# Attention prompt kernel: the last 512 tokens transposed by DMA, with the order of the start and the planner's table changed

## The chip, the core and the metric

The kernel runs on one core of one Trainium2 chip. The metric is the device time of one execution in microseconds: 803.9 us before the change, the median of three runs (802.73 to 804.06). TensorE (PE) multiplies, VectorE (DVE) and ScalarE (ACT) work element by element, GpSimd (POOL) helps, SyncE (SP) issues nearly all DMAs. Every engine runs its own list of instructions in order, and semaphores make one wait for another.

## What is computed

The inputs are x (2048 tokens of 640), two sets of weights and a gate vector, all bf16. Attention A is full softmax attention with 32 heads of 20; attention B is a local one, in which each token looks at 8 tokens at distances 0, 2, ... 14 before it. The result mixes both with a gate for each token. Cut to what matters:

```python
x = A_x
g = sigmoid((x * gate_w).sum(-1, keepdims=True))
# A: q, k, v = heads of x @ A_wqkv;  softmax(q k^T * 20**-0.5) v, heads joined, @ A_wo
# B: the same with B_wqkv, but keys and values only at s, s-2, ..., s-14; @ B_wo
out = g * A(x) + (1 - g) * B(x)
```

## The kernel before, in words

**Main loop.** A group is 512 queries of four heads (32 groups). For each group and each of 16 key blocks of 128 there are four score units, one for each head: 2048 units of 128 keys by 512 queries. Units are gathered into tiles of two or three. `qk` (L1616, matmuls L1629) fills a score buffer for a tile, `exp` (L1649, L1652) takes the exponential on ACT into one of five ebuf buffers, `pv` (L1661, matmuls L1693) multiplies with V into obank. Part of the units go round ACT: they ride along with a tile of two in its third bank, and DVE computes their exponential (L1642, then three shifts at L866 for a sum of four powers); such units come in quads of four (`wanted`, L1505, decides on each). There are two score buffers of three banks (`score[0]`, `score[1]`); the third bank of each, with a bank of its own called side 0, forms the pool of three side banks that all other matmul work shares. A tile of three units, or a tile with a rider, needs the third bank of its buffer.

**Planner.** The program is laid out by a planner that runs while it is built. `T(...)` puts a task with an estimated length on an engine's list; the estimates decide in which order tasks are placed, and nothing else. Between tiles, `spend` and `run_side` (L1284) take work from generators in order of priority: the V projection (`gen_v`, L762), K and Q projections of the other heads (`gen_kd`, `gen_qd`, `gen_q1`), constants such as KMd (`constants`, L515), the gate, attention B, the output folds. Where PE has nothing else, `filler` (L1700, matmuls L1714) inserts matmuls without use. `PLAN` (L50) is a table by tile number: at tile s it sets 21 parameters (slack, priorities, when to take a rider, filler share).

**The start, written out by hand.** SP issues the loads in this order: x in four parts of 512 tokens (the first in two halves), with wk0 (the K weights of the first four heads) after the first and wq0 (the Q weights of the first four heads) after the last, then WvA, WkA, gwT. x arrives with tokens on partitions and is needed with channels on partitions (`xT`). For every part `turn` (L1313, L1321) transposes on PE, 20 blocks of 128 by 128, into a score buffer, and `x_out` (L1334) evacuates it: ACT takes two of the five channel blocks (L1338), DVE three (L1341). `k_first` (L1355, L1348) projects K of the first four heads for one part, `k_max` (L1360, L1362) takes the maximum on DVE, `k_out` (L1366, L1369) writes kT on ACT. `q_half` (L1420, L1423) projects the queries of the first group; POOL pads their weights first (L558). The maxima of the four parts give a bound that enters the query by one more matmul (L1442, L1444). `v_first` and `v_out` (L1372, L1380) project V of the first key block into side 0 and copy it to vA on DVE. Then the generators start; `gen_v` (matmuls L592, copy L773) begins with block 1, since `NV0` is 1.

The banks for K by part are side 0, obank, side 0, and the third bank of score[1]. The B weights go into `stage` (L1461), over the space where the fourth part of x had landed.

Of the kernel before, what the change touches and what calls it, by code (L numbers as in the profile page):

```python
# [10 lines left out]
ALU = mybir.AluOpType  # L11
# [3 lines left out]
P = 128  # L15
S = 2048
D = 640
# [316 lines left out]
def _build(ctx, nc, A_x, A_wqkv, A_wo, B_wqkv, B_wo, gate_w, out):  # L334
# [33 lines left out]
    NE = 5  # L368
    NR = 2
    VW = TOK + 8  # L370
    NV0 = 1
    xT = sb([P, CN, S], BF16, "xT")
    WqP = sb([P, CN, P], BF16, "WqP")
    kvw = sb([P, 3 * CN * D], BF16, "kvw")
# [1515 lines left out]
```

## Time and profile before

| what | value |
|---|---|
| three runs, median (lowest, highest) | 803.9 us (802.73, 804.06) |
| profiled execution, own time | 802.24 us |
| its span in the profile | 800.4 us |
| ACT busy | 779.5 us (97%) |
| PE busy | 770.4 us (96%) |
| DVE busy | 717.6 us (90%) |
| POOL busy | 143.6 us (18%) |
| granted PE clock | 1.0 throughout |
| first exponential starts | 18.46 us |
| last exponential starts | 791.5 us |
| DMA share, 0 to 20 us | 0.95 |

Times inside the profile count from the start of the span. A line of the timeline gives start, length, engine, source line, operation, output and inputs by name, shape, how many were merged (x20) and, in brackets, the idle time before it with what ended it. A busy PE is not a PE at its peak, because matmuls are pipelined and their ends are modelled. SP's issuing and waiting are not counted as busy.

### The profile page before, as it was taken

Reading aid. Unit: us, or ns where it says so; the run is one execution under the profiler, and the core shown is the slowest. Engines: PE = TensorE matmul, PEld = TensorE weight load, DVE = VectorE, ACT = ScalarE, POOL = GpSimd, SP = SyncE. Lnnn points to the kernel's source line nnn. Section 1 sums busy time; section 2 is a strip of 40 time slices with the busy share of each in tenths; the row PEclk is TensorE's granted clock in tenths of the full one; section 3 lists DMA queues with packets and bytes.
Section 4 is the critical chain, followed back from the end, with each engine's and each line's share of the span. In section 5 each row is a group of like instructions: output and inputs, shape, how many; then the busy total and the mean of one; then the engine's idle time right before and its main releaser. Section 6 shows DMA issues by size and latency. Waiting matters only on the chain.

```text
span 800.4 us, 29142 instructions
## 1 busy us (share of the span) xinstructions
PE 770.4 (96%) x12193; PEld 274.6 (34%) x12194; DVE 717.6 (90%) x1291; ACT 779.5 (97%) x785; POOL 143.6 (18%) x239
## 2 busy tenths in 40 slices
PE   9999999999999999999999999999999999999997
PEld 5332223233333333432333334233333233333232
DVE  7567989999879999899989979999999988999995
ACT  5999999999999999999999999999999999999996
POOL 5004111105511211111111111111112111211110
PEclk9999999999999999999999999999999999999999
DMA  9101101012111301300122023022003001303001
GB/s 310 48 16 38 34 18 41 11 33 65 32 36 27 82 20 27 71 16 22 38 70 43 9 50 69 17 61 51 14 22 79 16 26 41 76 6 71 14 7 36
DMA packets 59446, 35.24 MB, mean 44 GB/s; under 512 B 25252, under 2 KB 58116, under 8 KB 59316
## 3 DMA queue, kind: packets, MB, share of 16 engines
q1 hardware_dynamic: 59028, 33.05, 16.7%
q8 instruction: 97, 1.59, 0.9%
q14 instruction: 33, 0.27, 0.1%
q10 hardware_dynamic: 288, 0.33, 0.1%
HBM read 11.45 MB, written 2.62 MB: 18 GB/s over the span
## 4 chain that ended last, share of the span: by engine, by line
PE 50%; ACT 30%; issue 12%; DVE 7%; ACTq 0%; DVEq 0%
ACT ebuf L1652 30%; PE score L1629 17%; PE obank L1693 14%; PE side L592 9%; PE score L592 4%; DVE uD L1642 3%; DVE uD L866 1%; PE side L1714 1%; PE obank L1714 1%; PE score L1321 1%; PE obank L493 1%; PE side L1050 1%; DVE stage L1036 0%; PE score L1714 0%; PE side L954 0%
## 5 line engine op out<-in xcount | busy, mean ns | idle before, releaser
L1652 ACT ACTIVATE ebuf<-score 128x1024 bf16<-128x1024 f32 (+1 forms) x750 | 766.9, 1192 | 4.7 <-PE score L1629 3.6
L1629 PE MATMUL score<-qT,kT 32*128 32x512 bf16 x2048 | 304.6, 384 | 21.3 <-ACT ebuf L1652 15.8
L1642 DVE TENSOR_SCALAR uD<-score 128x512 int16<-128x512 f32 x380 | 254.0, 680 | 23.7 <-PE score L1629 22.3
L866 DVE TENSOR_SCALAR uD<-uD 128x2048 int16<-128x2048 int16 x285 | 195.0, 701 | 7.0 <-PE obank L1693 6.3
L1629 PEld LDWEIGHTS score<-qT,kT 32*128 32x128 bf16 x2048 | 73.3, 91 | 275.7 <-ACT ebuf L1652 214.1
L1693 PE MATMUL obank<-ebuf,vA 128*21 128x512 bf16 x1668 | 164.8, 386 | 0.3 <-DVE oTt L806 0.2
L857 POOL TENSOR_TENSOR vS<-vA,vw 128x252 bf16<-128x252 bf16 x95 | 58.2, 613 | 472.1 <-DVE uD L866 320.4
L1693 PE MATMUL obank<-uD,vS 128*21 128x512 bf16 x1140 | 100.3, 380 | 0.0
L592 PE MATMUL side<-xT,kvw 128*32 128x256 bf16 (+1 forms) x1830 | 78.8, 284 | 0.2 <-DVE rQ L1015 0.2
L1693 PEld LDWEIGHTS obank<-ebuf,vA 128*21 128x21 bf16 x1668 | 40.8, 88 | 98.9 <-issue 77.7
L592 PEld LDWEIGHTS side<-xT,kvw 128*32 128x32 bf16 x1830 | 43.9, 96 | 29.1 <-issue 13.7
L1036 DVE TENSOR_TENSOR stage<-stage,eB 128x1280 bf16<-128x1280 bf16 x64 | 51.1, 815 | 0.0
L938 DVE TENSOR_TENSOR stage<-qkvB 128x1280 bf16<-128x1280 bf16 x64 | 50.9, 815 | 0.1
L824 POOL TENSOR_TENSOR oN<-oTt,rcp 128x256 bf16<-128x256 f32 (+1 forms) x61 | 38.4, 644 | 46.5 <-DVE uD L866 21.8
L592 PE MATMUL score<-xT,kvw 128*32 128x256 bf16 (+1 forms) x930 | 44.3, 296 | 0.0
L1693 PE MATMUL obank<-uD,vA 128*21 128x512 bf16 x380 | 35.3, 379 | 0.0
L922 DVE CAST qkvB<-side 128x512 bf16<-128x512 f32 (+1 forms) x51 | 29.2, 582 | 1.7 <-PE side L592 1.6
L1693 PEld LDWEIGHTS obank<-uD,vS 128*21 128x21 bf16 x1140 | 26.9, 90 | 11.1 <-issue 3.6
L592 PE MATMUL side<-woBp,oB 128*32 128x512 bf16 (+1 forms) x520 | 27.8, 308 | 0.5 <-DVE oB L1061 0.5
L592 PE MATMUL side<-woA_d,oTd 128*32 128x512 bf16 (+1 forms) x472 | 27.2, 310 | 0.0
L806 DVE STREAM_TRANSPOSE oTt<-obank 128x512 f32<-128x512 f32 x32 | 22.7, 708 | 4.4 <-PE obank L1693 4.3
L592 PEld LDWEIGHTS score<-xT,kvw 128*32 128x32 bf16 x930 | 21.0, 95 | 15.3 <-issue 10.7
(202 smaller groups left out, 542.6 us busy)
## 6 DMA issues: line engine op xcount, KB each, us to landing
stage<-qkvB SPq DMA_DIRECT2D x128, 82.5 KB, 2.2
stage<-in_B_wqkv_dram SPq DMA_DIRECT2D x1, 2400.0 KB
oTd<-oN SPq DMA_DIRECT2D x108, 20.0 KB
WqP<-in_A_wqkv_dram SPq DMA_DIRECT2D x13, 160.0 KB, 2.5
qT<-dst SPq DMA_DIRECT2D x104, 20.0 KB
out_dram<-outsb SPq DMA_DIRECT2D x12, 160.0 KB
kvw<-in_A_wqkv_dram SPq DMA_DIRECT2D x2, 800.0 KB
qT<-qbnd SPq DMA_DIRECT2D x72, 1.0 KB
```

The costliest lines, as they stand in the source:

```text
L592: ins = e.matmul(o[j:k, :], l(j) if callable(l) else l[:, j:k], r, start=(first and i == 0), stop=(last and i == n - 1), skip_group_check= ...
L806: T("dve", 0.623, lambda e: e.transpose(oTt[:, :], obank[:, :]), reads=["obank"], writes=["oTt"])
L824: T(en, c2 if half < 0 else 0.56, lambda e: e.tensor_tensor(oo, ii, ib, ALU.mult), reads=["rcp", "oTt"], writes=[("oN0", h) for h in ((0, ...
L857: T("pool", 0.62, lambda e: e.tensor_tensor(vS[:, d % NVS, :, :], _ap(vA, (kb * NQ + q) * 4 * DV, [[0, K - 1], [1, 4 * DV]]), _ap(vw, 0, [ ...
L866: T("dve", 0.066 + 0.1334 * n, lambda e, k=k: e.tensor_scalar(uD[u][:, 0:512 * n].bitcast(I16), uD[u][:, 0:512 * n].bitcast(I16), SHIFTS[k ...
L922: t = TB(dvc(n * TOK), lambda e, o=o, i=i: e.tensor_copy(o, i), reads=[("side", b)], writes=[key])
L938: TB(dvc(CN * TOK, 2), lambda e, w=w, ks=ks: e.tensor_tensor(prodB(w), qB[:, :, :], ks, ALU.mult), reads=["qB", "kB"], writes=[("prod", w) ...
L1036: TB(dvc(CN * TOK, 2), lambda e, o=o, vs=vs, ee=ee: e.tensor_tensor(o, vs, ee, ALU.mult), reads=["eB", ("prod", k)], writes=[("prod", k + ...
L1629: ins = e.matmul(o, kT[32 * j:32 * j + 32, q, kb * P:(kb + 1) * P], qT[g % NQT][32 * j:32 * j + 32, :], start=True, stop=True)
L1642: t = T("dve", 0.6, lambda e: e.tensor_scalar(uD[d % NU][:, 512 * i:512 * (i + 1)].bitcast(I16), side[x], UOFF, 0.0, op0=ALU.add, op1=ALU. ...
L1652: exps[s] = T("act", actc(512 * n), lambda e: e.activation(ebuf[s % NE][:, 0:512 * n], score[s % 2][:, 0:512 * n], ACTF.Exp, scale=LN2 / S ...
L1693: ins = e.matmul(obank[32 * j:32 * j + DV, :], v, src, start=(kb == 0), stop=(last and k >= len(lst) - 4), skip_group_check=True)
```

## The change

- The fourth part of x (tokens 1536 to 2047) no longer goes through `stage`, `turn` and `x_out`. Five DMAs, one for each 128 channels, read it transposed straight into xT. They stand at the same place in SP's queue, ahead of wq0.
- `k_first` of the fourth part moves ahead of that of the third, with its maximum. The banks change: the third part's K goes to the first bank of score[0], the fourth part's to side 0. Column and semaphore bookkeeping of the maxima follows: the third part's maximum is now the late one.
- `v_first` and `v_out` are no longer called. `NV0` is 0, so `gen_v` makes the first key block too, and bank 0 is marked free at the end of the first query.
- The load of the B weights waits for the fourth part of xT instead of for the reading of `stage` by the turn.
- The `PLAN` table is another one (61 rows before, the last at tile 740; the new one's last row is at tile 730).

```diff
 PLAN = {
-    0: ((0.3, 0.64), 0.39, 2.5, 2.5, 0.49, -1.3, -0.1, 11.8, 7.0, 7.2, 0.49, 0.47, 4.4, 4.0, 0.0, 0.75, 2, -3, 0.36, 4.0, 3.0),
...
-    740: ((0.3, 0.37), 0.31, 5.5, 6.6, 0.86, -1.01, -0.03, 14.7, 6.2, 9.68, 0.23, 0.79, 4.4, 4.23, 0.06, 0.72, 1, -3, 0.0, 4.0, 4.0),
+    0: ((0.39, 0.52), 0.32, 2.5, 2.5, 0.49, -1.3, -0.1, 11.8, 7.0, 7.2, 0.52, 0.47, 4.4, 4.0, 0.0, 0.75, 2, 0.0, 0.5, 4.0, 3.0),
...
+    730: ((0.48, 0.48), 0.28, 6.6, 5.5, 0.64, -1.3, -0.35, 11.8, 7.0, 7.37, 0.39, 0.47, 4.19, 2.8, 0.0, 0.79, 2, 0, 0.0, 4.0, 1.0),
 }
-    NV0 = 1
+    NV0 = 0
-    XOFF = [(oTd, 0), (oTd, 4 * D), (oB, 0), (stage, 2 * D * CN)]
+    XOFF = [(oTd, 0), (oTd, 4 * D), (oB, 0)]
...
-    x_load(3, 7.5)
+    T("sp", 8.5, lambda e: [e.dma_start(xT[:, c, 1536:2048], x_v[1536:2048, c * P:(c + 1) * P], transpose=True) for c in range(CN)],
+      writes=[("xT", 3, 0), ("xT", 3, 1)], dma=True, nd=CN, iss=0.5)
...
-    kbank = lambda tcc: ((side[0], ("side", 0)), (obank, "obank"), (side[0], ("side", 0)), (side[2], ("side", 2)))[tcc]
+    kbank = lambda tcc: ((side[0], ("side", 0)), (obank, "obank"), (score[0][:, 0:512], ("score", 0)), (side[0], ("side", 0)))[tcc]
...
+    KC = (0, 1, 3, 2)
...
-            kmx4[:, tcc:tcc + 1], kb_[:, :], AX.X, ALU.max, apply_absolute_value=True),
+            kmx4[:, KC[tcc]:KC[tcc] + 1], kb_[:, :], AX.X, ALU.max, apply_absolute_value=True),
...
     k_first(1)
-    turn(3)
     k_max(1)
-    x_out(3)
     k_out(1)
+    k_first(3)
+    k_max(3)
     k_first(2)
-    k_max(2)
-    k_first(3)
...
     q_half(0)
     q_half(1)
-    k_out(2)
+    k_out(3)
...
-    k_max(3)
+    k_max(2)
...
-    v_first()
-    t = k_out(3)
+    t = k_out(2)
...
-    v_out()
-    bank_free[0] = t.end + LAT["dve"] + 0.5
+    bank_free[0] = t.end
...
-    T("sp", 10.0, lambda e: e.dma_start(_ap(stage, 0, [[3 * D, CN], [1, 3 * D]]), wB_v[:, :, :]), writes=["stage", ("xs", 3)], dma=True, iss=2.0)
+    T("sp", 10.0, lambda e: e.dma_start(_ap(stage, 0, [[3 * D, CN], [1, 3 * D]]), wB_v[:, :, :]), reads=XT(3), writes=["stage"], dma=True, iss=2.0)
```

More of the change, by code (lines that the diff above doesn't have):

```diff
@@ L1429, in _build @@
     q_half(1)
-    k_out(2)
+    k_out(3)
     T("dve", 0.15, lambda e: e.tensor_reduce(kmx[:, 0:1], kmx4[:, 0:3], AX.X, ALU.max),
-      reads=[("kmx4", i) for i in range(3)], writes=[("kmx", 0)])
+      reads=[("kmx4", i) for i in (0, 1, 3)], writes=[("kmx", 0)])
     T("dve", 0.2, lambda e: e.tensor_scalar(KM3, KMmask, kmx[:, 0:1], None, op0=ALU.mult),
       reads=[("kmx", 0), "KMmask"], writes=["KM3"])
-    k_max(3)
+    k_max(2)
     T("dve", 0.25, lambda e: e.scalar_tensor_tensor(KM[0], KMmask, kmx4[:, 3:4], KM3, op0=ALU.mult, op1=ALU.min),
-      reads=[("kmx4", 3), "KMmask", "KM3"], writes=[("KM", 0)])
+      reads=[("kmx4", 2), "KMmask", "KM3"], writes=[("KM", 0)])
     T("act", actc(256), lambda e: e.activation(qabs[0][:, 256:512], side[1][:, 0:256], ACTF.Abs), reads=[("side", 1)], writes=[("qabs", 0, 1)])
```

121 rows, old and new, of the table PLAN are left out of this document.

## The prediction

> **What bounds the kernel now.** I read the page first: engine shares, then the costliest groups.
>
> ```profile
> span 800.4 us, 29142 instructions
> ...
> PE 770.4 (96%) x12193; PEld 274.6 (34%) x12194; DVE 717.6 (90%) x1291; ACT 779.5 (97%) x785; POOL 143.6 (18%) x239
> ...
> L1652 ACT ACTIVATE ebuf<-score 128x1024 bf16<-128x1024 f32 (+1 forms) x750 | 766.9, 1192 | 4.7 <-PE score L1629 3.6
> ```
>
> ACT does 750 exponentials (tiles) in 766.9 of the 800.4 us and sits idle before them for 4.7 us in all. By shape they are 580 of 1024 columns, 169 of 1536 and one of 512: 1668 units of 512 columns, at 766.9 / 1668 = 0.46 us each. The other 380 units go through DVE (L1642, x380), in quads of four. PE is nearly as full, but 592 of its matmuls are filler (L1714): 148 groups of four at about 0.22 us, some 32 us that can give way. So the end is: when the first exponential starts, plus ACT's work, plus ACT's holes, plus the tail. A microsecond won before the first exponential, or a hole closed, comes out whole at the end; work taken from PE or DVE in the middle does not.
>
> Second, the timeline of the first 24 us, since all of the diff but the table lies there; here PE alone from 10 to 16, and POOL's one wait. Columns: start, length, engine, line.
>
> ```profile
> 9.84 1.06 PE L1321 MATMUL score<-ident,oB 128*128 128x128 bf16 x16
> 10.99 1.02 PE L1348 MATMUL obank<-xT,kvw 128*128 128x512 bf16 x4
> 11.85 1.28 PE L1321 MATMUL score<-ident,stage 128*128 128x128 bf16 x20
> 12.97 1.24 PE L1348 MATMUL side<-xT,kvw 128*128 128x512 bf16 x5
> 14.27 1.24 PE L1348 MATMUL score<-xT,kvw 128*128 128x512 bf16 x5
> 15.35 0.71 PE L1423 MATMUL obank<-xT,WqP 128*128 128x256 bf16 x5
> ...
> 11.94 0.53 POOL L558 COPY WqP<-repB 128x400 bf16<-128x400 bf16 x1 [2.54 <-DMA repB<-in_A_wqkv_dram]
> ```
>
> PE goes from one to the next with no gap that matters, and the chain of work that ended last runs through it: 1.12 us of L1321 (the turn of the last 512 tokens) from 12.02, then 1.08 and 1.25 us of L1348 (K) to 15.53, then DVE's maximum. This stage is bound by PE.
>
> Third, the stretch after the first exponential.
>
> ```profile
> 18.46 1.45 ACT L1652 ACTIVATE ebuf<-score 128x1536 bf16<-128x1536 f32 x1 [0.49 <-PE score L1629]
> ...
> 18.84 0.96 DVE L519 TENSOR_SCALAR KMd<-outsb 128x160 bf16<-128x160 f32 x1
> ...
> 19.84 1.04 DVE L521 SCALAR_TENSOR_TENSOR KMd<-outsb,KMd 128x160 bf16<-128x160 f32 x1
> ...
> 20.80 0.48 DVE L773 CAST vA<-score 128x320 bf16<-128x320 f32 x1
> ...
> 21.33 0.60 PE L1629 MATMUL score<-qT,kT 32*128 32x512 bf16 x5 [1.05 <-DVE vA L773]
> 21.77 9.57 ACT L1652 ACTIVATE ebuf<-score 128x1536 bf16<-128x1536 f32 x8 [1.86 <-PE score L1629]
> ```
>
> Here is the largest hole: ACT idle 1.86 us before tile 1. Its third score bank holds the V projection of the second block, and DVE empties that bank late, behind two KMd instructions that take 0.96 and 1.04 us where the planner counts 0.25 each. That V block took this bank because bank 0 was still held by the first V projection (L1375, L1383).
>
> **The change, part by part.**
>
> *The turn goes.* On PE 1.12 us of the chain; on ACT 1.02 (L1338) and on DVE 0.96 (L1341) off the chain, worth nothing by themselves. Next late is the data itself, which K(3) now needs at 12.02.
>
> *When the last tokens land.* Now: the weights behind them (wq0, 640 packets of 160 bytes, 14 ns median in the packet record, 640 x 14 / 16 = 0.56 us on 16 engines) are in at 11.94, so the tokens are in by about 11.4. The 512 packets of 1280 bytes took 55 ns each: 1.76 us. I count the transposing form as rows of 128 elements, 512 x 5 = 2560 packets of 256 bytes. Nothing in this trace transposes in a DMA. Its plain 256-byte packets took 18 ns: 2560 x 18 / 16 = 2.88 us, 1.1 more: landing at 12.5. One end: no longer than now, 11.4. Other end: the rate of the 160-byte packets, 655 KB in 4096 x 14 / 16 = 3.6 us, landing 13.2. I take 12.5, the row with the same packet.
> The Trainium skill ("DMA: Bandwidth & Descriptors", Latency and other measured facts) gives DMA transposes an effective 261 GB/s with a non-contiguous middle dimension; 655 KB would then be an estimated 2.5 us, landing 12.15 and the gain below 1.0 instead of 0.65. No run here shows a transpose yet.
>
> *The start.* From 12.02 PE now needs 1.12 + 1.08 + 0.06 + 1.25 = 3.51 us to the last K. After: wait 0.48, then 1.08 + 1.25 + 0.06, together 2.87. Gain 0.65; ends 1.15 (lands at 11.4) and about 0 (13.2). K(2), now last, needs the evacuation of its turn, done at 12.87; it starts about 13.6, so that is hidden with 0.7 to spare. The rest (maximum, bound, query) keeps its order, so the first exponential moves from 18.46 to 17.8.
>
> *SP's queue.* Five issues stand where one of 0.51 us was, ahead of wq0, WvA, WkA and gwT. The plain issues beside it took 0.46 to 1.12; at 0.5 each these four go out 2 us later. That is hidden, because the 16 engines are busy without a break until 22 (share 0.94 or more in every microsecond from 3 on): a transfer issued at 4.33 landed at 11.94. What reaches the path is the longer transfer, 1.1: wq0 at 13.05, POOL's padding to 13.6, first needed by the query at 14.9: 1.3 of cover. WvA is now needed only after the first tile, WkA later. The B weights (L1461) waited on SP for the turn until 13.16; now they wait for the landing, 12.5; only the next WqP load stands behind.
>
> *K(2) in the first score bank.* New wait: tile 0's matmul needs ACT to have drained it. That drain stands where K(3)'s stands now (16.92 to 17.60, less 0.65), ahead of ACT's half of the query, for which tile 0 waits anyway. Nothing; cover 0.4.
>
> *First V projection back.* Its five matmuls (0.84 us, 0.69 of them on the chain that leads to the hole, but tile 0 at 18.02 waits for ACT's query, not for them) become 20 narrow ones (0.86) inside the stream, covered by the filler. The cast of 0.49 on DVE stays. The first product with V comes at 23.60, so there is room. But bank 0 is now free at once, so the first V block takes it, and the three-unit tile 1 no longer needs what DVE empties last. So I take the 1.86 us hole as gone. Ends: all of it stays (0), all gone (1.86). Next late would be tile 2 or 3, for DVE still starts its stream 1.5 us behind the plan; the removed cast at 18.13 gives it 0.49 back.
>
> *The table.* It sets slack, priorities and how many units ride on DVE. The trace cannot show the new schedule. Price: 4 units on or off ACT are 1.84 us. Each tile more or less with the same units is, at 766.9 less 1668 x 512 x 0.8334 ns (711.7) over 750, 0.07 us. The one hint in the diff is that the last row is 730 where it was 740, which fits fewer tiles but does not need it. I take 0, with two quads either way as ends, plus or minus 3.7.
>
> **Sum.** -0.65 - 1.86 + 0 = -2.5. The profiled execution took 802.24 us (span 800.4 and 1.8 around it), so 799.7 for the like of it; the median of the three runs is 803.9, 1.7 above that execution, and the forecast against it is 801.4.
>
> **Rivals.** About 0.2% (1.6 us) is what a measurement of this kernel can tell from no change: the runs of before spread by 1.3.
> - B, *the hole moves instead of closing.* For: DVE's two KMd instructions are unchanged and still four times their planned cost. Against: five ebuf buffers let ACT run ahead of V. Only the start counts: 803.9 - 0.65 = 803.2, within 0.2%.
> - C, *the table takes two more quads off ACT.* For: the last row; DVE idles 10% of the span, and 20 to 60 us is its emptiest stretch. Against: PE pays three more products per unit. -2.5 - 3.7: 797.7.
> - D, *the table leaves more on ACT.* For: two or three quads among 95 is a small difference between two schedules. From 2.2 quads on it eats the gain and 0.2% more: (2.5 + 1.6) / 1.84. Two to three quads: 805.1 to 806.9, slower.
> - E, *the transposes are late.* Place: PE's queue is in order and K(3) now stands ahead of K(2), so PE waits for the landing with ready work behind it. If each of the five issues cost SP what WkA's did (2.10), the last is out at 3.78 + 10.5 = 14.3 and in at about 16.5 (2.2 from issue to landing, the median of the stage loads). Then PE starts K(3) 4.5 late, less the turn's 1.1: +3.4, or +1.5 if the hole closes: 805.4 to 807.3. It costs the start from a landing at 13.1 on, and the whole from 15.0 on. Against: the plain issues of the same bytes beside it took 0.5 to 0.9.
>
> **Numbers.** The forecast (A) 0.42, spread 799.9 to 802.9; B 0.20; C 0.13; D 0.13; E 0.12. Faster: 0.36 of A, 0.13 of C, 0.02 of B, 0.51. Slower: D 0.13, 0.10 of E, 0.02 of B, 0.25. The rest, 0.24, within 0.2%. A's own range is 799.9 to 802.9; for 8 in 10 it must reach C's middle and into D and E: 797.5 to 806.8.
>
> **What would show it.** Right: no L1321 after 11; PE's wait before the third L1348 group near 0.5 us; first exponential near 17.8; no hole over 0.5 us before tiles 1 to 5; the exponentials' count and sum within 5 us of 750 and 767. Wrong in the start: that wait above 1.1. Wrong in the hole: a gap of one to two microseconds ended by a cast of vA. Wrong in the table: the count of L1642 away from 380 by eight or more, or holes in ACT later than 60 us.

## The result, and the profile after

The change made the kernel 0.7% slower. Over four runs each, the changed kernel took 809.05 us (808.33 to 809.51) against 803.55 us (802.73 to 804.06): a ratio of 1.0069, 95% interval 1.0051 to 1.0086. The forecast was 801.4, its range ended at 806.8. The profiled execution took 808.59 us, with a span of 806.8 where it was 800.4.

The page of the changed kernel, the three lines that answer to those of before (line numbers have moved by a few: the exponential is L1654, qk L1631, the rider L1644, the shift L870):

```profile
span 806.8 us, 29278 instructions
...
PE 766.0 (95%) x12300; PEld 276.6 (34%) x12301; DVE 713.5 (88%) x1276; ACT 780.5 (97%) x767; POOL 141.7 (18%) x237
...
L1654 ACT ACTIVATE ebuf<-score 128x1024 bf16<-128x1024 f32 (+2 forms) x733 | 769.2, 1221 | 8.6 <-PE score L1631 7.8
```

PE, DVE and POOL have less to do, ACT 1 us more, and the idle time ahead of the exponentials went from 4.7 to 8.6 us. So the 6.4 us of span divide thus: exponentials 769.2 - 766.9 = +2.3, holes ahead of them 8.6 - 4.7 = +3.9, start of the first one 18.44 - 18.46 = 0, rest +0.2.

By shape there are 521 exponentials of 1024 columns, 211 of 1536 and one of 512: 1676 units where 1668 were. Riders on DVE fell from 380 to 372. That is two quads more on ACT.

**The start.** PE from 10 to 16 us and the two lines of SP's queue around the transposes, changed kernel:

```profile
10.07 1.29 PE L1325 MATMUL score<-ident,oB 128*128 128x128 bf16 x20 [0.40 <-DMA oB<-in_A_x_dram]
11.42 1.03 PE L1352 MATMUL obank<-xT,kvw 128*128 128x512 bf16 x4
13.05 1.25 PE L1352 MATMUL side<-xT,kvw 128*128 128x512 bf16 x5 [0.61 <-DMA xT<-in_A_x_dram]
14.14 1.24 PE L1352 MATMUL score<-xT,kvw 128*128 128x512 bf16 x5
15.32 0.72 PE L1427 MATMUL obank<-xT,WqP 128*128 128x256 bf16 x5
```

```profile
3.94 7.46 SPq L475 DMA_TRANSPOSE xT<-in_A_x_dram  x5
11.45 0.58 SPq L477 DMA_DIRECT2D repB<-in_A_wqkv_dram  x1
```

Five issues held SP for 7.46 us, 1.49 each on average, where the plain load in the same place had taken 0.51. The transposed tokens are there at 13.05, 1.65 after the last issue, and PE waits 0.61 us for them. The third part of x (oB) came 0.40 too late for PE as well. wq0 went out at 11.45 instead of 4.33, so POOL's padding of it, which had begun at 11.94, began at 14.74 and ended at 15.27, just as the query was to start. The last K ends at 15.38 instead of 15.53, the query starts at 15.32 instead of 15.35, and between these two executions nothing is won.

That is one execution against one. In the three profiles that keep the start of before (the kernel before, e4, e5) the first exponential comes at 18.46, 18.72 and 19.28 us, and in five that keep the changed start (the changed kernel, e2, e3, e7, e8) at 18.05 to 18.65. A gain of a few tenths at the start is neither shown nor excluded.

**The first tiles.** The same stretch as in the prediction's third view:

```profile
18.44 1.45 ACT L1654 ACTIVATE ebuf<-score 128x1536 bf16<-128x1536 f32 x1 [0.49 <-PE score L1631]
20.45 2.37 ACT L1654 ACTIVATE ebuf<-score 128x1024 bf16<-128x1024 f32 x2 [0.55 <-PE score L1631]
22.98 3.71 ACT L1654 ACTIVATE ebuf<-score 128x1024 bf16<-128x1024 f32 x3 [0.16 <-PE score L1631]
```

The hole before tile 1 is 0.55 where it was 1.86. But the tile is another one, too: it has two units (1024 columns) here and had three (1536) before.

**A new place.** Between 65 and 75 us, by engine (ACT, POOL, DVE, and the one PE line that matters):

```profile
65.14 8.45 POOL L888 COPY kvw<-stage 128x640 bf16<-128x640 bf16 x5
66.03 1.50 DVE L870 TENSOR_SCALAR uD<-uD 128x2048 int16<-128x2048 int16 x1
68.05 2.95 DVE L870 TENSOR_SCALAR uD<-uD 128x2048 int16<-128x2048 int16 x2
70.92 1.39 DVE L719 TENSOR_SCALAR outsb<-dst 128x512 uint16<-128x512 uint16 x1
72.36 0.24 PE L733 MATMUL score<-outsb,KMd 128*32 128x128 bf16 x4 [2.70 <-DVE outsb L719]
73.74 1.30 DVE L870 TENSOR_SCALAR uD<-uD 128x2048 int16<-128x2048 int16 x2
74.05 2.37 ACT L1654 ACTIVATE ebuf<-score 128x1024 bf16<-128x1024 f32 x2 [4.01 <-PE score L1631]
```

While POOL copies B weights, the shifts of L870 take 1.5 us each; without it, at 73.74, two take 1.30. The absolute value at L719 takes 1.39. PE waits 2.70 us for it in the bound's product (L733), and because PE's list is in order, the score matmuls of the next tile stand behind. ACT is idle for 4.01 us. Here is the same place in the kernel before:

```profile
67.01 1.31 DVE L866 TENSOR_SCALAR uD<-uD 128x2048 int16<-128x2048 int16 x1
68.24 1.41 DVE L715 TENSOR_SCALAR outsb<-dst 128x512 uint16<-128x512 uint16 x1
69.70 0.24 PE L729 MATMUL side<-outsb,KMd 128*32 128x128 bf16 x4 [1.19 <-DVE outsb L715]
70.30 5.61 ACT L1652 ACTIVATE ebuf<-score 128x1024 bf16<-128x1024 f32 x5 [1.09 <-PE score L1629]
```

It was there already, with a hole of 1.09, and the prediction did not look at it. In the changed order more shifts stand between the start of POOL's copies and L719.

### The profile page after: what moved, and what is told of

Its sections match the earlier page's. It is cut to its first block, busy times and chain, and to the rows that moved or that the text cites. A ratio compares the mean times of both kernels' runs of the same rounds, so it can differ in the third digit from the quotient of the medians.

```text
span 806.8 us, 29278 instructions
## 1 busy us (share of the span) xinstructions
PE 766.0 (95%) x12300; PEld 276.6 (34%) x12301; DVE 713.5 (88%) x1276; ACT 780.5 (97%) x767; POOL 141.7 (18%) x237
## 4 chain that ended last, share of the span: by engine, by line
ACT 38%; PE 36%; issue 15%; DVE 9%; SPq 1%; DMA 0%; ACTq 0%; DVEq 0%
ACT ebuf L1654 38%; PE score L1631 12%; PE obank L1695 10%; PE side L596 9%; PE score L596 2%; DVE uD L870 2%; DVE uD L1644 2%; SPq L475 1%; DVE stage L1040 1%; PE obank L1716 1%; DVE stage L942 1%; PE score L1716 1%; ACT eB L989 0%; PE side L1054 0%; DMA xT<-in_A_x_dram 0%
## 5 line engine op out<-in xcount | busy, mean ns | idle before, releaser
L1654 ACT ACTIVATE ebuf<-score 128x1024 bf16<-128x1024 f32 (+2 forms) x733 | 769.2, 1221 | 8.6 <-PE score L1631 7.8
L1631 PE MATMUL score<-qT,kT 32*128 32x512 bf16 x2048 | 293.7, 384 | 26.4 <-ACT ebuf L1654 21.5
L1644 DVE TENSOR_SCALAR uD<-score 128x512 int16<-128x512 f32 x372 | 249.2, 681 | 30.1 <-PE score L1631 28.4
L870 DVE TENSOR_SCALAR uD<-uD 128x2048 int16<-128x2048 int16 x279 | 193.3, 709 | 6.3 <-PE obank L1695 5.3
L1631 PEld LDWEIGHTS score<-qT,kT 32*128 32x128 bf16 x2048 | 71.2, 91 | 270.4 <-ACT ebuf L1654 210.5
L596 PE MATMUL side<-xT,kvw 128*32 128x256 bf16 (+1 forms) x2380 | 104.9, 288 | 1.4 <-DVE qkvB L638 0.5
L596 PEld LDWEIGHTS side<-xT,kvw 128*32 128x32 bf16 x2380 | 56.1, 96 | 38.9 <-issue 17.9
L926 DVE CAST qkvB<-side 128x512 bf16<-128x512 f32 (+1 forms) x62 | 36.0, 590 | 3.4 <-PE side L596 3.0
L820 POOL TENSOR_TENSOR rcp<-rcp,gA 128x16 f32<-128x16 f32 x31 | 6.9, 223 | 122.1 <-DVE rcp L814 69.0
L596 PE MATMUL side<-kvw,xT 128*32 128x320 bf16 x560 | 25.5, 301 | 1.2 <-DVE vA L777 1.1
L596 PE MATMUL side<-woA_d,oTd 128*32 128x512 bf16 (+2 forms) x500 | 26.5, 301 | 0.0
L596 PE MATMUL side<-woBp,oB 128*32 128x512 bf16 (+1 forms) x540 | 25.6, 298 | 0.1
```

Source lines behind the costliest of these rows:

```text
L596: ins = e.matmul(o[j:k, :], l(j) if callable(l) else l[:, j:k], r, start=(first and i == 0), stop=(last and i == n - 1), skip_group_check= ...
L870: T("dve", 0.066 + 0.1334 * n, lambda e, k=k: e.tensor_scalar(uD[u][:, 0:512 * n].bitcast(I16), uD[u][:, 0:512 * n].bitcast(I16), SHIFTS[k ...
L926: t = TB(dvc(n * TOK), lambda e, o=o, i=i: e.tensor_copy(o, i), reads=[("side", b)], writes=[key])
L1631: ins = e.matmul(o, kT[32 * j:32 * j + 32, q, kb * P:(kb + 1) * P], qT[g % NQT][32 * j:32 * j + 32, :], start=True, stop=True)
L1644: t = T("dve", 0.6, lambda e: e.tensor_scalar(uD[d % NU][:, 512 * i:512 * (i + 1)].bitcast(I16), side[x], UOFF, 0.0, op0=ALU.add, op1=ALU. ...
L1654: exps[s] = T("act", actc(512 * n), lambda e: e.activation(ebuf[s % NE][:, 0:512 * n], score[s % 2][:, 0:512 * n], ACTF.Exp, scale=LN2 / S ...
```

## The experiments

The theory after these readings: most of the loss is the 4-us hole, caused by POOL's copies slowing DVE; two quads more on ACT are the rest; the transposes themselves cost nothing at the end. The rivals: the transposes are the cause; or the new order as a whole is longer and single places mean little. Ratios are against the kernel before on the same chip. Unless it is said otherwise, an experiment keeps the order of its kernel instruction by instruction, and only the edit differs. Line numbers move by a few from kernel to kernel; a profile has those of its own run.

**e1: the transposes alone, on the kernel before.** The fourth turn and its evacuation are dropped; order of K, first V and table stay.

```diff
-    x_load(3, 7.5)
+    five DMAs with transpose=True into xT[:, c, 1536:2048]
-    turn(3)
-    x_out(3)
```

> The kernel before, its order of instructions kept everywhere, with one edit: the five transposing DMAs stand in place of the fourth load, and its turn on PE and its evacuation are taken out; K's order, the first V projection and the table stay. Theory T (the 5.5 us come from the schedule that the new table makes, not from the start): the last tokens land near 13.05 and the query weights near 14.7 as in the changed kernel, the query is projected from about 15.3 as before, the first exponential starts within 0.6 of 18.46, and the time is 803.5, give or take 1. Rival R (the transposes and what they hold up cost the time): 806 to 809.

Measured: 802.70, ratio 0.9996 (0.9987 to 1.0005). No difference that can be measured, so the transposes are not what made the change slower. SP was held even longer here, 8.11 us for the five. The profiled execution began its prelude late by another delay (0.96 us of waiting for the padded wk0), so its first exponential came at 19.15, outside the 0.6 us around 18.46 that was expected, and cannot be set against 18.46 as an effect of the edit.

**e2: the changed kernel with POOL's five copies out of the way.** They are moved from 65 us to just behind POOL's rows of ones, which end at about 21 us; in this run they start at 26.95, when the load of the B weights has come in.

```diff
+    for a_, t_ in zip([ones[NQ - 1]] + bw[2], bw[2]):   # ones: L1403, bw[2]: five of L888
+        move(t_, a_)                                    # t_ right behind a_ on its engine
```

> The changed kernel, its order kept on all engines but POOL: the five copies of the third part of the B weights (L888), which run beside DVE from 65 to 74 us, move up on POOL to right behind its last row of ones, near 21 us. Theory T, with its part H (the hole of 4.0 us at 70 us is DVE slowed by POOL's copies, 1.47 instead of 0.69 us a shift, with PE waiting behind): L870 back at 0.69 there, L719 at 0.29, the hole under 1.5, the time 809.05 less 2.5 to 3.5, 805.5 to 806.5. If the hole is in the order of the instructions itself (PE's list waits for a bound whatever DVE takes): hole 2.5 to 4, 808 to 809. R: 809, hole unchanged.

Measured: 805.61, ratio 1.0034 (1.0021 to 1.0046), 3.4 us less than the changed kernel by the medians and 2.8 by the ratios. The place in this kernel:

```profile
67.33 1.27 DVE L870 TENSOR_SCALAR uD<-uD 128x2048 int16<-128x2048 int16 x2
68.53 0.28 DVE L719 TENSOR_SCALAR outsb<-dst 128x512 uint16<-128x512 uint16 x1
69.16 0.23 PE L733 MATMUL score<-outsb,KMd 128*32 128x128 bf16 x4
70.52 1.29 DVE L870 TENSOR_SCALAR uD<-uD 128x2048 int16<-128x2048 int16 x2
70.83 5.12 ACT L1658 ACTIVATE ebuf<-score 128x1024 bf16<-128x1024 f32 x5 [0.67 <-PE score L1635]
```

The same two shifts take 1.27 instead of 2.95, the absolute value 0.28 instead of 1.39, PE no longer waits, and the hole is 0.67 instead of 4.01. The 3.3 us taken from the hole come out at the end. What is left above the kernel before, 805.61 - 802.94 = 2.7, is about as much as the 2.3 us of exponentials; that the one causes the other is not shown by this run, and e3 speaks against it.

**e3: the changed kernel with eight units fewer on ACT.** Eight exponentials of 1536 columns, between tiles 300 and 600, do only their first 1024; the third unit is left out and its sum is wrong.

```diff
-            ebuf[s % NE][:, 0:512 * n], score[s % 2][:, 0:512 * n], ACTF.Exp, ...
+            ebuf[s % NE][:, 0:512 * nn], score[s % 2][:, 0:512 * nn], ACTF.Exp, ...   # nn = 2 in eight tiles
```

> The changed kernel, same order; eight tiles of three units between tile 300 and 600 take the exponential of two units only, so eight units of 512 columns are left out of ACT. Theory T (ACT sets the end, so the eight units that the new table leaves on it count whole): 8 x 0.43 = 3.4 us less, 805.6. Rival (in the middle PE or DVE sets the pace): less than 1 us, 808 to 809.

Measured: 808.78, ratio 1.0073 (1.0059 to 1.0087), where the changed kernel had 1.0069. The 8 x 0.43 = 3.4 us did not come out. Its exponentials:

```profile
L1660 ACT ACTIVATE ebuf<-score 128x1024 bf16<-128x1024 f32 (+2 forms) x733 | 766.6, 1209 | 11.5 <-PE score L1631 10.5
```

ACT's work fell by 2.6 us, its idle time rose by 2.9. Part of that is the hole at 70 us, 5.21 in this execution where the changed kernel had 4.01. Just behind that hole its exponentials start 1.49 us later than the changed kernel's; at the last one this is 0.68, so 0.8 us of the 3.4 was kept. PE's list is unchanged, so taking work from ACT without laying out PE anew gave little here. This speaks against reading "+2.3 us of exponentials" as a cause by itself; what two quads fewer would give in an order laid out for them was not run.

**e4: the kernel before, with the three constant instructions on DVE moved back.** L518, L519 and L521 (the KMd constants) go behind L674.

```diff
+    for a_, t_ in zip(q1t + cst, cst):   # q1t: L674, cst: L518, L519, L521
+        move(t_, a_)
```

> The kernel before, its order kept but for three instructions of DVE: the cast and the two KMd instructions (L518, L519, L521) move behind the query of group 1 (L674), so that the V cast (L773) which empties tile 1's third bank comes first. Theory of the hole (DVE is 2.3 us late with that bank): ACT's 1.86 us before tile 1 falls under 0.5, nothing new of that size appears, and the time is 803.55 less 1.2 to 1.8, about 802.0. Rival (the hole moves to a later tile, as rival B of the prediction has it): 803 to 803.6.

Measured: 801.71, ratio 0.9986 (0.9977 to 0.9995). From the timeline of this kernel, ACT and DVE:

```profile
20.92 3.71 ACT L1658 ACTIVATE ebuf<-score 128x1536 bf16<-128x1536 f32 x3 [0.74 <-PE score L1635]
...
23.26 0.24 DVE L521 TENSOR_SCALAR KMd<-outsb 128x160 bf16<-128x160 f32 x1
23.54 0.33 DVE L523 SCALAR_TENSOR_TENSOR KMd<-outsb,KMd 128x160 bf16<-128x160 f32 x1
```

The two KMd instructions (L521 and L523 in this kernel) take 0.24 and 0.33 where they took 0.96 and 1.04. There POOL was copying rows of ones (4.01 us from 16.69), here it is quiet. The hole shrinks from 1.86 to 0.74, less far than expected (under 0.5), and the time falls by about as much, 1.1 to 1.2 us. That these instructions stood ahead of the V cast is thus shown to make most of the hole. That POOL made them long is read from the two timelines: here the instructions were moved, and no run moved the copies of ones away from them. It fits the place at 70 us, where e2 moved POOL alone.

**e5: both moves, on the kernel before.** e4, and the five POOL copies moved up as in e2 (behind the constants' last memset).

```diff
+    for a_, t_ in zip(q1t + cst, cst):
+        move(t_, a_)
+    for a_, t_ in zip([ones[NQ - 1]] + bw[2], bw[2]):
+        move(t_, a_)
```

> The kernel before with two moves: the three KMd instructions behind the query of group 1 (as in e4), and on POOL the five copies of the third part of the B weights up from 65 us to right behind the last row of ones, waiting there for the last mask of DVE's constants (near 30 us), so that they run while DVE does little. Theory H (wherever POOL copies run beside DVE's instructions, these take two to five times as long; there is nothing else to the holes): the hole of 1.09 us at 70 us falls under 0.3, and the time is that of e4 (0.9986 of before) less 0.8 to 1.1: 0.9975 of before, near 801. Rival (the copies slow something else at 30 us, or the hole at 70 has another cause): no better than e4, 0.9986 or more.

Measured: 800.33, ratio 0.9969 (0.9958 to 0.998): faster than both kernels. The hole at 70 us is gone: one run of sixteen exponentials goes from 61.40 to 78.89 without idle time. Of the 2.5 us, 1.1 are e4's; the rest, 1.4, is the 1.09 of that hole and 0.3 more that no line was found for.

**e6: the changed kernel with wq0 issued ahead of the transposes.**

```diff
+    l.remove(lq0)
+    l.insert(l.index(xl3), lq0)   # lq0: load of wq0, xl3: the five transposes
```

> The changed kernel, with one edit on SP: wq0 (the query weights) is issued ahead of the five transposing DMAs instead of behind them. Theory Q (the start's gain was lost to SP's 7.46 us of issue, which holds wq0 back to 14.74): the wait of POOL for wq0 ends before 13, but the last tokens land 0.6 later (13.6), so PE waits that much longer for them and the first exponential stays within 0.3 of 18.44; the time stays within 0.5 of the changed kernel's. Rival (wq0 alone holds the start): first exponential 0.4 earlier, 808.6.

Measured: 810.27, ratio 1.0095 (1.0081 to 1.0109), above the changed kernel by 1.2 us by the medians and 2.1 by the ratios. POOL could pad wq0 at 10.69 already, as expected, but otherwise neither expectation came true. SP and PE:

```profile
4.34 8.53 SPq L475 DMA_TRANSPOSE xT<-in_A_x_dram  x5
...
14.54 1.25 PE L1352 MATMUL side<-xT,kvw 128*128 128x512 bf16 x5 [1.87 <-DMA xT<-in_A_x_dram]
```

The last transpose leaves SP at 12.87 and the tokens are in at 14.54, 1.67 later, as they were 1.65 later in the changed kernel. With transposes, the tokens arrive at a nearly fixed time after SP has got rid of the fifth issue: 1.56 to 1.80 us in the other five profiles of the changed kernel and its variants where PE waits for them (e2, e3, e7, e8, e11). The first exponential starts at 19.81, 1.37 later than in the changed kernel, and about that comes out at the end. The order of the change (transposes first) was the better of the two.

**e7 and e8: the filler.** In both, the filler matmuls of the changed kernel have 64 columns instead of 512; e7 also leaves out e3's eight units.

```diff
-                ins = e.matmul(o[32 * j:32 * j + 32, :], ..., xT[:, 0, 0:512], ...)
+                ins = e.matmul(o[32 * j:32 * j + 32, 0:64], ..., xT[:, 0, 0:64], ...)
```

> As e3 (eight units of ACT left out between tiles 300 and 600 of the changed kernel), and every filler matmul of PE has 64 columns instead of 512, all else the same. Theory P (e3 gave back only 0.9 of 3.4 us because PE's list is fixed and its 182 filler groups of 0.22 us are in it whether ACT is early or not): the eight units now count nearly whole against the changed kernel with small filler (e8), 2.5 to 3.4 less. Rival (another part of PE's order or DVE sets the pace there): 1 or less between the two.

> The changed kernel with every filler matmul at 64 columns instead of 512, all else the same: some 30 us less of PE's busy time. Theory P: PE's list is the pacer in places only; 0.5 to 2 us less than the changed kernel, 807 to 808.5, with the granted clock unchanged. Rival 1 (filler stands only where PE waits anyway): no change. Rival 2 (without filler the granted clock falls): slower, and the clock below 0.99.

Measured: e7 816.39, ratio 1.0170 (1.0156 to 1.0184); e8 816.24, ratio 1.0176 (1.0150 to 1.0202). The granted clock was 0.975 and 0.981 where the changed kernel had 0.999. The page of e8, its filler and its exponentials:

```profile
PEclk9999899999999999999999999999999999999969
...
L1716 PE MATMUL side<-xT,ident 128*32 128x64 bf16 x308 | 9.5, 207 | 0.0
...
L1654 ACT ACTIVATE ebuf<-score 128x1024 bf16<-128x1024 f32 (+2 forms) x733 | 769.7, 1231 | 13.7 <-PE score L1631 12.9
```

PE had less to do and was later: ACT waited 12.9 us for scores instead of 7.8. It waits where the clock is low: from 772 to 784 us the granted clock is 0.50 in e8 and ACT is busy for 10.57 of 12 us; in the changed kernel it is 1.00 there, and ACT is busy throughout. The Trainium skill ("TensorE: Matmul & The Clock Gate", Part 1: The HAM clock gate) says that the clock is throttled by default and activity releases it; the granted clock of the three runs moves that way with the filler.

No gain of the eight units is seen between e7 and e8 either, but e8's four runs lie between 814.23 and 820.61, and with another clock the pair does not test what it was made for.

**e9: five plain loads in place of the five transposes**, with the same rows of 256 bytes. The last 512 tokens are then not transposed, and what is computed of them is wrong.

```diff
-  e.dma_start(xT[:, c, 1536:2048], x_v[1536:2048, c * P:(c + 1) * P], transpose=True)
+  e.dma_start(_ap(xT, c * S + 1536, [[P, 4], [1, P]]), x_v[1536:2048, c * P:(c + 1) * P].rearrange("(b p) d -> p b d", p=P))
```

> The changed kernel with its five transposing DMAs replaced by five plain loads from the same rows of x into the same places of xT, each a 512 by 128 block as [128, 4, 128] in rows of 256 bytes; the last 512 tokens of x are thus not transposed, so what is computed of them is other data. Theory Q (it is the transposing that holds SP for 1.5 us an issue): each of the five takes about 0.5 us on SP, as the plain stage load of the kernel before did (0.51), the load of wq0 is issued near 6.5 instead of 11.45, WqP's copy starts near 12 and the first exponential near 17.6. Rival (any DMA with this many packets holds SP so long): the five still take 1.4 us or more each, wq0 near 11, and the first exponential stays near 18.4. In both the hole near 70 us of 4 us stays and the whole time is within 2 us of the changed kernel's 809.

Measured, one run: 809.79. SP and PE of this kernel:

```profile
3.89 6.04 SPq L475 DMA_DIRECT2D xT<-in_A_x_dram  x5
9.98 0.52 SPq L477 DMA_DIRECT2D repB<-in_A_wqkv_dram  x1
...
12.90 1.25 PE L1352 MATMUL side<-xT,kvw 128*128 128x512 bf16 x5 [0.34 <-DMA xT<-in_A_x_dram]
```

Between the two expectations, and nearer to the rival; the first exponential, at 18.18, lies between them as well. The five plain issues took 0.51, 1.55, 0.72, 1.49 and 1.60; the five transposing ones of the changed kernel 2.14, 1.25, 1.39, 1.26 and 1.26. So five plain loads of these rows hold SP for most of that time too, and about 1.4 of the 7.46 us is what the transposing adds. How long an issue takes is no property of the load alone, however: the loads of WkA (L476) and gwT (L478) took 2.10 and 2.47 in the kernel before, where they stood close behind the loads of x, and 0.53 each in the changed kernel, from 12.64 on (L480, L482). Whether the size of the rows, the number of loads or what is still under way ahead of them makes the difference was not taken apart.

The data arrives only 0.15 earlier than with transposes, though the last issue ends at 9.93, 2.97 before. So without the transposing, SP's issuing alone does not set the arrival.

PE does not wait for the third part of x in this run. That is no effect of the transposes: with a plain load behind that part, PE waited 0.50 and 0.52 us for it in e4 and e5 and not at all in the kernel before and here; with transposes behind it, 0.39 to 0.42 in the changed kernel, e1, e2, e3, e6 and e8, and not at all in e7.

**e10 and e11: the tables crossed.** The new table on the kernel before, and the old one on the changed kernel; everything is laid out anew from them, so these two do not keep an order.

```diff
-PLAN = { the table of its own kernel }
+PLAN = { the table of the other one }
```

> The kernel before in all but the table, which is that of the change; everything is planned anew from it. Theory F (a table fits only the start that it was searched for, the two are one change): the planner then takes fewer quads off ACT, 360 riders by its own list against 380, so 5 quads of four 512-column units stay on ACT, 20 times 0.43 = +8.6 us of exponentials, and the rest of the order is another too: slower by 8 us or more, beyond 811. Rival (the table by itself is worth about what the account of the change shows, two quads and a hole): 803 to 809.

> The changed kernel in all but the table, which is that of the kernel before; planned anew. Theory F: 324 riders by the planner's own list against 372, so 12 quads more on ACT, 48 times 0.43 = +20.6 us of exponentials, slower than the changed kernel: beyond 820. Rival (the old table is the better one, and the new one the cost of the change): at or below the kernel before, 800 to 805.

Measured, one run each: 855.63 and 858.90. The exponentials of e10, then those of e11:

```profile
L1655 ACT ACTIVATE ebuf<-score 128x1024 bf16<-128x1024 f32 (+2 forms) x733 | 775.4, 1226 | 38.9 <-PE score L1632 38.0
```

```profile
L1651 ACT ACTIVATE ebuf<-score 128x1024 bf16<-128x1024 f32 (+1 forms) x716 | 788.5, 1306 | 35.9 <-PE score L1628 35.2
```

Exponentials rise by 8.5 and by 19.3 us over the kernel that each was made from, as expected from 360 and 324 riders, and the holes ahead of them by 34 and 27 us, which was not. Each of these two tables fits only the start that it came with. Table and start are one change; the question "what did the table cost" has no answer by swapping it.

The two runs do answer another question, why the hole before tile 1 shrank. ACT at tile 1, in e10 and in e11:

```profile
20.97 2.37 ACT L1655 ACTIVATE ebuf<-score 128x1024 bf16<-128x1024 f32 x2 [0.34 <-PE score L1632]
...
23.29 15.99 ACT L1651 ACTIVATE ebuf<-score 128x1536 bf16<-128x1536 f32 x15 [2.38 <-PE score L1628]
```

With the new table tile 1 has two units, and the hole is 0.34 though the first V projection still holds bank 0. With the old table it has three, and the hole is 2.38 though bank 0 is free. So what closed most of the hole came with the table, and not with the freed bank; the size of tile 1 is the difference that these lines show.

## Why the prediction was wrong, step by step

| step | forecast | measured |
|---|---|---|
| first exponential (two profiles) | -0.65 | 0 |
| hole before tile 1 | -1.86 | -1.31 |
| ACT's work (table) | 0 | +2.3 |
| hole at 70 us | not in the sum | +2.9 |
| other holes and rest | 0 | +2.5 |
| span | -2.5 | +6.4 |

The step that decided is the table. It priced the new order by its quads alone, at 0, and neither it nor the sum had a term for a hole later than 60 us; the runs show a hole of 4.01 us at 70 us where 1.09 had been, and 2.3 us more of exponentials. The start failed as well, on SP's queue, but e1 shows that this did not make the change slower.

**What bounds the kernel: right in its frame, wrong in two clauses.** The loss does lie in ACT's work and ACT's holes. Holes come out nearly whole (e2: 3.3 of hole, 2.8 to 3.4 at the end; e4: 1.1 and 1.1). Work taken from ACT does not, as long as PE's list stays the same (e3: 3.4 taken, 0.8 of it kept, nothing seen in the time). And the filler is not "some 32 us that can give way": cut to 64 columns, it made the kernel slower than the changed one by 7 us by the medians and 9 by the ratios (e8), with ACT waiting where the granted clock was 0.50.

**When the last tokens land: mis-sized, and by the wrong mechanism.** Forecast 12.5, measured 13.05, close to the late end of 13.2, where the step itself said a gain of about 0. The packet rates used are not what set it: the last issue ended at 11.40, and e6 shows the landing following the fifth issue again, by 1.67 us. They were not far off all the same: the plain loads of e9, which left SP at 9.93, came in at 12.90. The rate of 261 GB/s from the Trainium skill ("DMA: Bandwidth & Descriptors", Latency and other measured facts), with its estimate of 12.15, was further off.

**SP's queue: this step failed first.** The prediction says: "at 0.5 each these four go out 2 us later. That is hidden, because the 16 engines are busy without a break until 22". The issues took 1.49 each, wq0 went out 7.1 us later, and the engines were not busy: their share was 0.67 from 11 to 12 us and 0.45 from 12 to 13. The cover of 1.3 us for the padding was used up to the last tenth. Rival E had the place and the mechanism. Its price of 2.1 an issue was too high; with 1.49 an issue its own sum gives 3.78 + 7.46 + 2.2 = 13.4, against 13.05 measured. By its own point (from 13.1 on the start suffers) it decided nothing at the end, and e1 confirms that.

**The start.** The turn's 1.12 us did go. 0.43 was given back before the third K began, nearly all of it in the wait for the third part of x; 0.61 was the wait for the tokens, 0.13 more than reckoned. With the 0.06 between the K groups, which went too, that leaves 0.15 at the last K; the query gained 0.03, for its first weights waited for the late padding. The prediction's upper end of 1.15 is 1.12 by its own terms. It also took one profile's start for fixed, and there is 0.8 us between the starts of the three profiles that share it.

**K(2) in the first score bank: right.** The first exponential still waits 0.49 for its scores, as before.

**The V projection back: right in size by luck.** The hole lost 1.31 of its 1.86 us, but not because bank 0 was free: with the old table and a free bank it is 2.38 (e11), with the new table and the bank taken 0.34 (e10). The prediction had tile 1 keep its three units; the new table gave it two, which need no third bank. The cause of the hole was read only halfway, too: the prediction named the KMd instructions at "four times their planned cost" but not why. In the kernel before, POOL was copying beside them; in e4, where it was not, they are short. The place at 70 us could have been found the same way, for the same thing stands there in the profile of before (L715 at 1.41 us, with 1.09 of hole).

**The table: the step that decided; the value taken as 0 was wrong, its price right.** Two quads more on ACT, 2 x 1.84 = 3.7, less 17 tiles at 0.07 = 1.2, gives 2.5; the busy time rose by 2.3. That is the upper end named there and short of rival D's 2.2 quads, so by work alone the change would have been slower than the forecast but not clearly slower than before. What decided was the order that came with the table: with POOL's copies moved away from the place at 70 us, 2.8 to 3.4 us of the loss go (e2). "Holes in ACT later than 60 us" was listed as the sign of a wrong table, and the page of after shows it; but no term of the sum and no rival stood for it. Both ends of the table step counted quads alone.

**What stays open.** The last 2.5 us of the account are small holes (0.60, 0.27, 0.39, 0.43 and others) and a tail longer by 0.5; no run took them apart, nor is it shown how much of the 2.3 us of exponentials comes out at the end. The hole at 70 us has two sizes, and they go with the clock. It is 4.01 in the changed kernel and in e6, where the granted clock stays at 1.00 behind PE's wait; it is 5.21, 5.33, 5.29 and 5.35 in e3, e7, e8 and e9, where the clock from 73 to 74 us is 0.50 and the eight matmuls of pv behind the wait take 0.93 to 1.07 us instead of 0.60. What decides between the two was not tried.

## What to carry to other kernels

A kernel whose order is laid out from estimates has as its weak places the spots where the estimates are furthest off: search the profile of before for instructions that take several times their usual length, ask what ran beside them, and expect a new order to land on them again. A new order has to be priced with its holes, not only with its work. When a term comes out right, ask whether its mechanism did: here a tile had changed its size. And the cost of issuing a DMA is taken from a row with like rows and like company, for the same load took SP 0.53 or 2.47 us by its place; the queue's own time can set the arrival.

## What the hardware showed that was not expected

- **DVE beside POOL.** Some instructions from SBUF to SBUF were two to five times as long while POOL copied: L870 0.64 and 1.47 us, L719 0.28 and 1.39, the KMd pair 0.24 and 0.33 against 0.96 and 1.04. Others were not: the maximum of L641 took 0.69 beside POOL (72.94) and without (76.19) in the changed kernel. The cast of vA, which reads PSUM, took 0.49 in both cases (18.13 beside POOL and 22.78 without, in the kernel before). The Trainium skill ("SBUF — State Buffer", SBUF: two separate sides) describes a pair of ports that the two engines share, DVE for some of its instructions only, under an exclusive lock, so that the later one waits for the other's whole instruction. The trace agrees as far as it goes: the longest delay, 1.11 us, is below the length of one POOL copy (8.45 / 5 = 1.69).
- **Issues.** Five transposes of 512 by 128 held SP for 7.43 to 9.07 us in eight profiles, five plain loads of the same rows for 6.04 in one; one load of 512 rows of 1280 bytes took 0.51. The load of gwT took 2.47 close behind the loads of x and 0.53 later.
- **The start varies.** With the same order of instructions up to it, the first exponential came at 18.46, 18.72 and 19.28 us in three profiles, with PE waiting for the third part of x in the later two (0.50 and 0.52) and not in the first.
- **Filler.** With the filler at 64 columns instead of 512, the granted clock went from 0.999 to 0.981 and 0.975.
- **A wait and the clock.** Behind PE's wait of 2.7 to 2.9 us at 70 us the granted clock was 1.00 in two profiles and 0.50 in four.
